# First scores as four 64x32 array tiles issued together, wider third score tile and row-0 product, one matmul for both halves of the gate weights

## The chip, the cores and the metric

The kernel runs on one core of a Trainium2 chip. Its measure is the device time of one launch in microseconds (us): a median over runs, and beside it one execution that was recorded by the profiler. TensorE (PE in the rows) multiplies, VectorE (DVE), ScalarE (ACT) and GpSimd (POOL) work elementwise, SyncE (SP) issues most of the DMAs. Each engine works through its own instruction stream in order and waits on semaphores for the others.

## The reference, cut to what matters

Three stages follow each other: an attention with 32 packed queries per head, a Fourier mixing with a two-layer network, and a mixture of eight experts with one expert per token.

```python
# 8 batches, 8 heads, 576 tokens, head_dim 64, 32 packed queries p
p_packed = sm_attn(p, k, v)                 # first softmax: 32 rows against 576 keys
x = sm_attn(q, p_packed, p_packed)          # second softmax: 576 rows against 32 keys
...
X = np.fft.fft(np.fft.fft(x, axis=1), axis=2)
u = x + np.real(X)                          # then a normalisation of every row
u = u + np.maximum(un @ w_ch1, 0) @ w_ch2   # 512 -> 2048 -> 512
...
logits = u @ w_gate                         # 8 experts, and one column more: w_local
local_gate = sigmoid(u @ w_local)
e = argmax(logits) if s == 0 or local_gate < 0.5 else e_of_the_token_before
out = p[e] * (np.maximum(u @ w1[e], 0) @ w2[e])    # 512 -> 1024 -> 512
```

## The kernel before, in words

**Numbers.** Nearly all products are made of float16 halves: a value is split into hi and lo, and three products (`PASS`: hi*hi, hi*lo, lo*hi) are summed in PSUM. The first scores are the exception: they are float32 matmuls, and each of these shows in the trace as two MATMUL records.

**The generators.** `attention(b)` yields step by step the first softmax, the second softmax, the transforms along channels and sequence, and the normalised rows of one batch. `Mix` is the two-layer network of one group of 512 tokens (256 for the groups "R0" and "R1"): `mm1(f)` makes twelve matmuls into `hp`, `mm2(f)` twelve into the four accumulators `acc`. While the mixing of batch b runs, `tick()` advances `attention(b + 1)`, the splitting of the channel weights (`cw`) and of the expert weights (`ew`: load `se`, split into `so` on ACT at L264 and DVE at L265, write to DRAM), and `after_mix` (scaled rows `xh`, gate logits). At the end come routing and 41 expert blocks (`e1`, `e2`).

**What sets the order.** The code is emitted in that interleaved order, and a scheduler then orders each engine's stream by priority, which is the place of emission; `tc.high_priority(offset=...)` moves instructions forward by so many places. `SOON` is 200 and is given to `greatest` and `exps` of the first softmax; `scores` has offset 0. Tiles of a pool take the slot that comes free, and the first writer of a reused slot waits for the last reader of the old tile.

**The two PSUM slots of `att`.** The pool `psA` has two buffers, which all of these share: the first scores `s1_b_hf_i`, the products `pps`, `ptp`, `s2`, `gp`, `bp`, `zd`, the row tiles `P`, `Q`, `X` of the transforms (`P` of the last 32 slots is read by ACT at L626 and by DVE at L630 to L642, its `X` by DVE at L652), and the logits `lp`. For batch 0 two of three tiles come from `psO` instead.

**The first softmax.** `pt` holds the packed queries of two heads as a block-diagonal 128x64 stationary operand. `scores(hf)` (L367) makes four float32 matmuls of 288 columns, one for each key half i and each pair of heads p2; the outputs of p2 = 0 and 1 stand in partitions 0-63 and 64-127. `greatest` takes maxima on DVE (L378 to L380), `exps` the exponentials on ACT (L385), `turn` casts, splits and transposes by DMA into `et`, which `pps` (L430) multiplies with the values.

**The second scores.** `scores2(i)` (L479) takes the slots in tiles of 128, 128 and 99 (three times the last 32 slots and slot 0), with the queries as stationary operand. `zd` (L572) is the product for row 0, with a stationary operand `zt` of 64 columns. `logits` (L767) makes twelve matmuls of 9 columns a token tile: four row chunks by three passes.

Of the kernel before, what the change touches and what calls it, by code (L numbers as in the profile page):

```python
# [25 lines left out]
RB = 3  # L26


def runs(n):
    """the block of every step: RB runs of blocks take turns, each with weights of its own"""  # L30
    size = [len(range(r, n, RB)) for r in range(RB)]
    return np.array([s // RB + sum(size[:s % RB]) for s in range(n)])


def tokmap():
    """natural token of each (column, partition) of the token tiles"""
# [12 lines left out]
def prep(inputs):  # L49
    """Lays the inputs out for the kernel; the constants depend on shapes alone."""  # L50
# [15 lines left out]
    last = np.concatenate([np.r_[256:288, 0]] * 3)      # the last slots and slot 0, three times  # L66
    o["qd"] = pairs_T(qn[:, :, np.concatenate([np.r_[0:256], last, np.r_[288:544], last + 288])])
    o["kd"] = pairs_T(heads(k))
    pt = pairs_T(heads(p))
    pd = np.zeros((NB, 128, 4, 64), f)  # L70
    pd[:, :64, :, :32] = pt[:, :64]
    pd[:, 64:, :, 32:] = pt[:, 64:]
    o["pd"] = pd
# [20 lines left out]
    # constants from the shapes  # L94
# [27 lines left out]
    c3 = np.zeros((128, 3), f)                          # of the last slots' rows: sign, shift, part  # L122
# [11 lines left out]
    c16[:, 0] = pp[:, None] < pp[None, :]              # strictly earlier rows  # L134
# [48 lines left out]
def _build(tc, nc, ctx, A, stop):  # L183
# [42 lines left out]
    zt = ap.tile([128, 2, 2, 64], F16, name="zt")  # L226
# [40 lines left out]
    def ch_weights():  # L267
        for f in range(16):
# [10 lines left out]
            if srcs[0].dtype == I32:  # L279
                # float64 words to float32: the exponent's three spare bits go, the mantissa keeps 23  # L280
# [18 lines left out]
    def expert_weights():  # L299
        for e in range(NE):  # L300
            for k in range(8):
                # the rows of w1, then those of w2
# [4 lines left out]
                for a in range(2):  # L307
                    so = wp.tile([128, 2, 512], F16, tag="so", name=f"so{e}_{k}_{a}", bufs=2)
                    # no faster than the groups go
# [8 lines left out]
    def attention(b):  # L318
# [8 lines left out]
        def spare(f, n):  # L327
            # room that the weights need later
            return w2h[:, f:f + 3].rearrange("p f a n -> p (f a n)")[:, :n]
# [23 lines left out]
        pt = ap.tile([128, 4, 64], F32, tag="pt", name=f"p{b}")  # L353
# [13 lines left out]
        def scores(hf):  # L367
            s1[hf] = [att(f"s1_{b}_{hf}_{i}") for i in range(2)]
            for i in range(2):
                for p2 in range(2):  # L370
                    nc.tensor.matmul(s1[hf][i][64 * p2:64 * p2 + 64, :288], pt[:, 2 * hf + p2, :],  # L371
                                     kts[hf][:, p2, 288 * i:288 * i + 288], start=True, stop=True)
            (load_v if b else load_q)(hf)
# [23 lines left out]
        for steps in (((scores, 0),), ((greatest, 0),), ((exps, 0), (scores, 1)), ((turn, 0), (greatest, 1)),  # L397
                      ((exps, 1),), ((turn, 1),)):
            for fn, hf in steps:
                with tc.high_priority(offset=SOON if fn in (greatest, exps) else 0):  # L400
                    fn(hf)
# [36 lines left out]
        # every head's own block, divided by the sum  # L438
# [16 lines left out]
        # second softmax, the slots n in tiles of 128, 128 and three times the last 32 and n = 0  # L455
# [4 lines left out]
        # along the channels  # L460
# [18 lines left out]
        def scores2(i):  # L479
            s2 = s2s[i] = att(f"s2_{b}_{i}")  # L480
            for pr in range(4):
                for lu in range(2):
                    c0, j0 = 355 * lu + 128 * i, 256 * lu + 64 * pr
                    for n, (x, y) in enumerate(PASS):
                        nc.tensor.matmul(s2[:nrs[i], j0:j0 + 64], qts[pr // 2][:, x, pr % 2, c0:c0 + nrs[i]],
# [63 lines left out]
        # along the sequence  # L549
        qs0 = ap.tile([128, 576], F32, tag="f32w", name=f"qs{b}_0", bufs=4)  # L550
        for k, (cs, hf) in enumerate(((0, 0), (0, 1), (1, 0), (1, 1))):
# [14 lines left out]
            if k == 2:  # L566
                # row 0: the odd slots' part of P, and what the slots' mean adds
                zd = att(f"zd{b}")
                n = 0
                for hf in range(2):  # L570
                    for (x, y) in PASS:
                        nc.tensor.matmul(zd[:64, :257], zt[:, hf, x], g[:, hf, y, 0], start=n == 0, stop=n == 5)  # L572
                        n += 1
# [3 lines left out]
        for t in (2, 0, 1) if b % 4 == 3 else (0, 1, 2):  # L577
# [76 lines left out]
            if t < 2:  # L654
# [3 lines left out]
                if t == 0 and b % 4 != 3:  # L658
                    # the rest runs beside the next tile
# [58 lines left out]
    class Mix:  # L718
        """one group of tokens: tiles are (U tile, column) of each 128 tokens"""
# [44 lines left out]
    def after_mix(tiles):  # L764
        xt = None

        def logits(col):  # L767
            lp = att(f"lp{col}")
            n = 0
            for c in range(4):  # L770
                for (x, y) in PASS:
                    nc.tensor.matmul(lp[:, :9], xt[:, 4 * x + c], wgh[:, c, y], start=n == 0, stop=n == 11)
                    n += 1
            nc.vector.tensor_scalar(LG[:, col], lp[:, :9], RSC[:, col:col + 1], 2.0 ** -20, ALU.mult, ALU.mult)
# [29 lines left out]
    def choose(gr, rp):  # L804
        """experts of the tokens of four batches, and their weights"""
# [77 lines left out]
        # the weight of the chosen expert, with the scales of the token's row  # L883
# [14 lines left out]
    def place(nm, ncol, b0, nb, early, rp):  # L898
        """blocks b0 .. b0+nb-1 from the tokens of the first ncol columns that are not taken"""
# [28 lines left out]
        # expert of every block  # L928
# [17 lines left out]
        # position of every token  # L946
# [6 lines left out]
        if early:  # L953
# [13 lines left out]
            # the tokens placed here leave the later placement  # L967
# [14 lines left out]
        # the tokens of the slots  # L982
# [253 lines left out]
```

## Time and profile before

| what | value |
|---|---|
| runs: median (lowest to highest) | 1546.48 us (1542.96 to 1549.28), 3 runs |
| profiled execution, first to last instruction (span) | 1548.2 us |
| PE busy | 1422.9 us (92%), 8452 matmul records |
| DVE busy | 771.0 us (50%) |
| ACT busy | 478.3 us (31%) |
| POOL busy | 334.5 us (22%) |
| mean granted TensorE clock, share of full | 0.964 |

The profiled execution has no other time than its span; it lies within the range of the runs. "Busy" is the union of an engine's records. A matmul's record is longer than its share of the stream, since its drain overlaps the next one; so the time that a matmul takes from PE is read from the distance between starts. A row of the timeline merges equal instructions: start, length, engine, line, operation, tiles, count, and in brackets the idle time before it with what ended it. In the rows a tile's buffer numbers are left out: `s` is a score tile of either softmax, told apart by its line.

### The profile page before, as it was taken

Reading aid. Unit: us, or ns where it says so; the run is one execution under the profiler, and the core shown is the slowest. Engines: PE = TensorE matmul, PEld = TensorE weight load, DVE = VectorE, ACT = ScalarE, POOL = GpSimd, SP = SyncE. Lnnn points to the kernel's source line nnn. Section 1 sums busy time; section 2 is a strip of 40 time slices with the busy share of each in tenths; the row PEclk is TensorE's granted clock in tenths of the full one; section 3 lists DMA queues with packets and bytes.
Section 4 is the critical chain, followed back from the end, with each engine's and each line's share of the span. In section 5 each row is a group of like instructions: output and inputs, shape, how many; then the busy total and the mean of one; then the engine's idle time right before and its main releaser. Section 6 shows DMA issues by size and latency. Waiting matters only on the chain. (4 is left out here: it accounts for less than half of the span.)

```text
span 1548.2 us, 23197 instructions
## 1 busy us (share of the span) xinstructions
PE 1422.9 (92%) x8452; PEld 705.5 (46%) x8452; DVE 771.0 (50%) x1547; ACT 478.3 (31%) x892; POOL 334.5 (22%) x332
## 2 busy tenths in 40 slices
PE   4597898998999899999899899999799999989996
PEld 3243444544465454454454456554354344434442
DVE  6778967567564766765766756343441111111110
ACT  4264434335233433533433433211111111111111
POOL 4347414104110410410410420001111121212111
PEclk6589999999999999999999999999999999999999
DMA  8375447457465744836736646244977969897686
GB/s 266 72 231 152 132 109 209 113 138 224 111 167 125 226 118 137 224 104 158 205 105 165 173 123 162 80 164 124 274 181 152 291 134 219 192 318 168 134 201 171
DMA packets 319732, 261.35 MB, mean 169 GB/s; under 512 B 254783, under 2 KB 266175, under 8 KB 318976
## 3 DMA queue, kind: packets, MB, share of 16 engines
q1 hardware_dynamic: 313056, 239.65, 59.5%
q0 software_dynamic: 6560, 20.19, 4.6%
q8 instruction: 67, 1.10, 0.3%
q14 instruction: 49, 0.40, 0.1%
HBM read 267.91 MB, written 53.74 MB: 208 GB/s over the span
## 5 line engine op out<-in xcount | busy, mean ns | idle before, releaser
L753 PE MATMUL acc<-w2h,ht 128*128 128x512 f16 x1728 | 418.4, 382 | 0.6 <-DVE ul L761 0.6
L733 PE MATMUL hp<-ut,w1h 128*128 128x512 f16 x1536 | 377.1, 385 | 6.4 <-DMA ut<-unh 3.5
L733 PEld LDWEIGHTS <-w1h 128*128 128x128 f16 x1920 | 185.0, 99 | 193.7 <-issue 27.1
L753 PEld LDWEIGHTS <-ht 128*128 128x128 f16 x1728 | 165.9, 99 | 195.8 <-issue 22.3
L1098 PE MATMUL ehp<-w1b,xgt 128*128 128x512 f16 x984 | 230.0, 381 | 8.2 <-DMA w1b<-WS 5.8
L1117 PE MATMUL eo<-w2b,hx 128*128 128x512 f16 x984 | 227.4, 381 | 8.7 <-DMA hx<-hb 8.7
L1106 DVE SCALAR_TENSOR_TENSOR hb<-ehp,hb 128x512 f16<-128x512 f32 x82 | 56.7, 691 | 351.4 <-ACT hb L1105 333.9
L741 DVE SCALAR_TENSOR_TENSOR ht<-hp,ht 128x512 f16<-128x512 f32 (+1 forms) x160 | 101.6, 635 | 199.2 <-ACT ht L740 198.4
L1117 PEld LDWEIGHTS <-hx 128*128 128x128 f16 x984 | 95.8, 98 | 126.9 <-DMA hx<-hb 13.9
L1098 PEld LDWEIGHTS <-xgt 128*128 128x128 f16 x984 | 95.7, 98 | 125.4 <-issue 7.1
L264 ACT ACTIVATE so<-se 128x512 f16<-128x512 f32 x128 | 79.8, 627 | 189.8 <-DMA WS<-so 151.6
L740 ACT ACTIVATE ht<-hp 128x512 f16<-128x512 f32 (+1 forms) x160 | 87.4, 547 | 154.6 <-PE hp L733 154.4
L265 DVE SCALAR_TENSOR_TENSOR so<-se,so 128x512 f16<-128x512 f32 x128 | 112.1, 883 | 9.4 <-ACT so L264 9.0
L1124 POOL DMA_INDIRECT out<-ys,sidx x41 | 41.5, 1013 | 326.6 <-ACT ys L1123 291.6
L1123 ACT ACTIVATE ys<-eo,scl 128x512 f32<-128x512 f32 x41 | 28.2, 687 | 266.5 <-PE eo L1117 266.5
L350 POOL TENSOR_TENSOR qh<-q,qh 128x1420 f16<-128x1420 f32 x15 | 43.8, 2921 | 283.9 <-ACT qh L349 281.1
L1068 POOL DMA_INDIRECT xg<-XS,gidx x41 | 42.3, 1031 | 188.2 <-DVE sidx L1024 105.1
L1105 ACT ACTIVATE hb<-ehp 128x512 f16<-128x512 f32 x82 | 48.9, 597 | 105.3 <-PE ehp L1098 105.0
L371 PE MATMUL s<-k,p 128*64 128x288 f32 x128 | 41.1, 466 | 14.6 <-DVE ru L642 9.0
L733 PE MATMUL hp<-utr,w1h 128*128 128x256 f16 x384 | 47.1, 272 | 0.8 <-DVE ht L741 0.8
L557 PE MATMUL bp<-cst,eh 128*128 128x289 f16 (+1 forms) x192 | 35.4, 327 | 13.5 <-ACT eh L534 8.0
L688 POOL TENSOR_TENSOR unh<-un,unh 128x512 f16<-128x512 f32 x32 | 38.1, 1201 | 31.5 <-ACT unh L687 30.2
(287 smaller groups left out, 1388.8 us busy)
## 6 DMA issues: line engine op xcount, KB each, us to landing
w1b<-WS SPq DMA_DIRECT2D x156, 512.0 KB
w2b<-WS SPq DMA_DIRECT2D x156, 512.0 KB
se<-in_w SPq DMA_DIRECT2D x64, 512.0 KB
WS<-so SPq DMA_DIRECT2D x128, 256.0 KB
sw<-in_wc SPq DMA_DIRECT2D x32, 512.0 KB
q<-in_qd SPq DMA_DIRECT2D x16, 710.0 KB
v<-in_vd SPq DMA_DIRECT2D x16, 640.0 KB
k<-in_kd SPq DMA_DIRECT2D x16, 576.0 KB
```

The costliest lines, as they stand in the source:

```text
L264: nc.scalar.activation(dst_hi, src, AF.Copy, scale=scale)
L265: nc.vector.scalar_tensor_tensor(dst_lo, src, scale, dst_hi, ALU.mult, ALU.subtract)
L350: nc.gpsimd.tensor_tensor(qh[:, 1], qt, qh[:, 0], op=ALU.subtract)
L733: nc.tensor.matmul(hp[:, :ntok], w1h[:, f, c, x], ut[:, 4 * y + c, :ntok], start=n == 0, stop=n == 11)
L740: nc.scalar.activation(ht[:, 0, :ntok], hp[:, :ntok], AF.Relu)
L741: pace[0] = nc.vector.scalar_tensor_tensor(ht[:, 1, :ntok], hp[:, :ntok], 0.0, ht[:, 0, :ntok], ALU.max, ALU.subtract).ins
L753: nc.tensor.matmul(self.acc[j], ht[:, x, 128 * j:128 * j + 128], w2h[:, f, y], start=f == 0 and n == 0, stop=f == 15 and n == 2)
L1068: nc.gpsimd.indirect_dma_start(out=g_, out_offset=None, in_=XS[0:rows], in_offset=bass.IndirectOffsetOnAxis(ap=gidx[:, b:b + 1], axis=0), ...
L1098: nc.tensor.matmul(hp, xt[b][:, 4 * x + c], w1b[b % RB][:, 2 * c + fg, y], start=n == 0, stop=n == 11)
L1105: nc.scalar.activation(h[:, fg, :512], hp, AF.Relu)
L1106: nc.vector.scalar_tensor_tensor(h[:, fg, 512:], hp, 0.0, h[:, fg, :512], ALU.max, ALU.subtract)
L1117: nc.tensor.matmul(op, h[:, f // 4, 4 * x + f % 4], w2b[b % RB][:, f, y], start=n == 0, stop=n == 23)
```

## The change

The first scores use `pt` without the zeros: four matmuls of 64 rows and 32 columns in place of two of 128 rows and 64 columns, for each key half. Head r of a pair stands in rows 64r to 64r+63, its output in partitions 64*p2 + 32*r; so the four use two row halves and four column strips, and all write one PSUM tile. `scores` gets the offset `SOON`. The third score tile is computed over 128 columns (29 of them belong to neighbouring slots and are not read), for which the columns of `qd` are laid in another order. `zt` and the row-0 product have 128 columns. The logits take hi and lo of the gate weights as one operand of 18 columns for the hi rows and 9 columns for the lo rows; DVE then adds the two halves. Comments were removed throughout.

```diff
-    o["qd"] = pairs_T(qn[:, :, np.concatenate([np.r_[0:256], last, np.r_[288:544], last + 288])])
+    o["qd"] = pairs_T(qn[:, :, np.concatenate([np.r_[0:256], last + 288, last, np.r_[288:544]])])
...
-    pd = np.zeros((NB, 128, 4, 64), f)
-    pd[:, :64, :, :32] = pt[:, :64]
-    pd[:, 64:, :, 32:] = pt[:, 64:]
-    o["pd"] = pd
+    o["pd"] = pairs_T(heads(p))
...
-    zt = ap.tile([128, 2, 2, 64], F16, name="zt")
+    zt = ap.tile([128, 2, 2, 128], F16, name="zt")
...
-        pt = ap.tile([128, 4, 64], F32, tag="pt", name=f"p{b}")
+        pt = ap.tile([128, 4, 32], F32, tag="pt", name=f"p{b}")
...
             for i in range(2):
                 for p2 in range(2):
-                    nc.tensor.matmul(s1[hf][i][64 * p2:64 * p2 + 64, :288], pt[:, 2 * hf + p2, :],
-                                     kts[hf][:, p2, 288 * i:288 * i + 288], start=True, stop=True)
+                    for r in range(2):
+                        d, row = slice(64 * r, 64 * r + 64), 64 * p2 + 32 * r
+                        nc.tensor.matmul(s1[hf][i][row:row + 32, :288], pt[d, 2 * hf + p2],
+                                         kts[hf][d, p2, 288 * i:288 * i + 288], start=True, stop=True)
...
-                with tc.high_priority(offset=SOON if fn in (greatest, exps) else 0):
+                with tc.high_priority(offset=SOON if fn in (scores, greatest, exps) else 0):
...
-                    c0, j0 = 355 * lu + 128 * i, 256 * lu + 64 * pr
+                    c0, j0 = ((0, 128, 355), (454, 582, 256))[lu][i], 256 * lu + 64 * pr
                     for n, (x, y) in enumerate(PASS):
-                        nc.tensor.matmul(s2[:nrs[i], j0:j0 + 64], qts[pr // 2][:, x, pr % 2, c0:c0 + nrs[i]],
+                        nc.tensor.matmul(s2[:, j0:j0 + 64], qts[pr // 2][:, x, pr % 2, c0:c0 + 128],
...
-                        nc.tensor.matmul(zd[:64, :257], zt[:, hf, x], g[:, hf, y, 0], start=n == 0, stop=n == 5)
+                        nc.tensor.matmul(zd[:, :257], zt[:, hf, x], g[:, hf, y, 0], start=n == 0, stop=n == 5)
...
             for c in range(4):
-                for (x, y) in PASS:
-                    nc.tensor.matmul(lp[:, :9], xt[:, 4 * x + c], wgh[:, c, y], start=n == 0, stop=n == 11)
-                    n += 1
-            nc.vector.tensor_scalar(LG[:, col], lp[:, :9], RSC[:, col:col + 1], 2.0 ** -20, ALU.mult, ALU.mult)
+                nc.tensor.matmul(lp[:, :18], xt[:, c], wgh[:, c].rearrange("p y e -> p (y e)"), start=c == 0, stop=False,
+                                 skip_group_check=True)
+                nc.tensor.matmul(lp[:, :9], xt[:, 4 + c], wgh[:, c, 0], start=False, stop=c == 3, skip_group_check=True)
+            lsum = wp.tile([128, 9], F32, tag="lsum", name=f"lsum{col}", bufs=2)
+            nc.vector.tensor_reduce(lsum, lp[:, :18].rearrange("p (y e) -> p e y", y=2), axis=AX.X, op=ALU.add)
+            nc.vector.tensor_scalar(LG[:, col], lsum, RSC[:, col:col + 1], 2.0 ** -20, ALU.mult, ALU.mult)
```

The offset moves the scores on PE. Before, the scores of batch 3 stand in the mixing of group 8 (batch 2), third product of `mm1`; each float32 matmul stands between two of the mixing's:

```order
L733 MATMUL hp8_2_3160<-ut2_2809,w1h_127 128x512
L371 MATMUL s1_3_0_0_3176<-k3_0_3172,p3_3169 64x288
L733 LDWEIGHTS w1h_127
L733 MATMUL hp8_2_3160<-ut2_2809,w1h_127 128x512
L371 MATMUL s1_3_0_0_3176<-k3_0_3172,p3_3169 64x288
```

After, they stand in the last product of the group before it (`hp4_15`), twelve matmuls `acc4` to `acc7` behind the transform's last row tiles `P2_2` and `X2_2`:

```order
L753 MATMUL acc7_2049<-w2h_128,ht4_12_2913 128x512
L370 MATMUL s1_3_0_0_3192<-k3_0_3188,p3_3185 32x288 x4
L733 LDWEIGHTS w1h_127
L733 MATMUL hp4_15_3078<-ut1_1693,w1h_127 128x512
...
L370 MATMUL s1_3_0_1_3193<-k3_0_3188,p3_3185 32x288 x4
...
L370 MATMUL s1_3_1_0_3238<-k3_1_3190,p3_3185 32x288 x4
L370 MATMUL s1_3_1_1_3239<-k3_1_3190,p3_3185 32x288 x4
```

Four matmuls of the mixing stand between the first two groups of scores, seven between the second and the third, none between the third and the fourth. Batches 5, 6 and 7 have the same order; in batch 2 ten matmuls stand ahead of the first group, and two between it and the second; batch 4's scores move by half a product only. The first group writes the slot of `P2_2`, the second that of `X2_2`, the third and fourth the slots of the first two.

On ACT the copy of `P2_2` (`qs2_2`) and the exponentials of batch 3 stand like this before:

```order
L264 ACTIVATE so1_0_0_3067<-se1_0_3050 128x512
L626 COPY qs2_2_3045<-P2_2_3016 32x257
L264 ACTIVATE so1_0_1_3084<-se1_0_3050 128x512
L264 ACTIVATE so1_1_0_3209<-se1_1_3167 128x512
L740 ACTIVATE ht4_15_3080<-hp4_15_3062 128x512
L264 ACTIVATE so1_1_1_3247<-se1_1_3167 128x512
```

and after:

```order
L260 ACTIVATE so1_0_0_3083<-se1_0_3066 128x512
L626 COPY qs2_2_3061<-P2_2_3032 32x257
L260 ACTIVATE so1_0_1_3100<-se1_0_3066 128x512
L260 ACTIVATE so1_1_0_3229<-se1_1_3183 128x512
L384 ACTIVATE e32_3_0_3235,sums3_3187<-s1_3_0_0_3192,mx3_0_3217 128x288
L384 ACTIVATE e32_3_0_3235,sums3_3187<-s1_3_0_1_3193,mx3_0_3217 128x288
```

The splits `so` of the expert weights stay ahead of the copy; the exponentials now come behind the third of them, ahead of `ht4_15`.

## Rows read from the trace of the kernel before

**Rows 1.** Stretch: length; PE, PEld, DVE, ACT, POOL busy (records); clock, DMA share, GB/s.
```profile
217.00:332.00 115.00, 109.57 (x712) 54.09 (x710) 74.40 (x143) 44.38 (x84) 24.19 (x24) 0.99 0.58 157
```

**Rows 2.** Timelines of ACT, PE, DVE behind the last row tiles of batch 2.
```profile
314.46 0.63 ACT L264 ACTIVATE so<-se 128x512 f16<-128x512 f32 x1 [2.00 <-DMA WS<-so]
320.87 0.63 ACT L264 ACTIVATE so<-se 128x512 f16<-128x512 f32 x1 [3.08 <-DMA WS<-so]
315.14 2.54 PE L733 MATMUL hp<-ut,w1h 128*128 128x512 f16 x11
316.87 0.41 DVE L642 TENSOR_TENSOR ru<-P,qs 32x256 f32<-32x256 f32 x1
```

**Rows 3.** Timeline of PE, scores of batch 2 in steady mixing.
```profile
216.75 0.70 PE L371 MATMUL s<-k,p 128*64 128x288 f32 x2
217.39 0.39 PE L733 MATMUL hp<-ut,w1h 128*128 128x512 f16 x1
217.71 0.70 PE L371 MATMUL s<-k,p 128*64 128x288 f32 x2
```

**Rows 4.** Timeline of PE, all scores of batch 0, at the lower clock.
```profile
5.50 4.18 PE L371 MATMUL s<-k,p 128*64 128x288 f32 x16 [5.50 <-DMA k<-in_kd]
```

**Rows 5.** Timeline of PE, column tiles and two score matmuls side by side.
```profile
63.79 0.28 PE L609 MATMUL X<-pph,big 128*32 128x256 f16 x2
64.00 0.71 PE L371 MATMUL s<-k,p 128*64 128x288 f32 x4
```

**Rows 6.** Timeline of PE, second scores of batch 1.
```profile
121.60 1.56 PE L485 MATMUL s<-pth,qh 128*128 128x64 f16 x48
126.89 1.27 PE L485 MATMUL s<-pth,qh 128*99 128x64 f16 x24
```

**Rows 7.** Timeline of PE, one logits product; then DVE's group that reads them.
```profile
856.63 0.45 PE L772 MATMUL lp<-wgh,xt 128*128 128x9 f16 x12
856.94 2.75 PE L733 MATMUL hp<-ut,w1h 128*128 128x512 f16 x12
L774 DVE TENSOR_SCALAR LG<-lp,RSC 128x9 f32<-128x9 f32 x36 | 7.8, 217 | 12.0 <-PE lp L772 11.8
```

**Rows 8.** Groups of PE by form: the row-0 product.
```profile
L572 PE MATMUL zd<-g,zt 128*64 128x257 f16 x48 | 7.4, 295 | 1.1 <-DVE zt L564 1.1
```

**Rows 9.** Timelines of PE and DVE at the same place of batches 1, 5, 6.
```profile
199.83 0.38 PE L733 MATMUL hp<-ut,w1h 128*128 128x512 f16 x1
200.76 0.40 DVE L642 TENSOR_TENSOR ru<-P,qs 32x256 f32<-32x256 f32 x1
...
700.89 2.75 PE L733 MATMUL hp<-ut,w1h 128*128 128x512 f16 x12
704.67 0.40 DVE L642 TENSOR_TENSOR ru<-P,qs 32x256 f32<-32x256 f32 x1
...
815.68 2.54 PE L733 MATMUL hp<-ut,w1h 128*128 128x512 f16 x11
817.51 0.41 DVE L642 TENSOR_TENSOR ru<-P,qs 32x256 f32<-32x256 f32 x1
```

**Rows 10.** Timeline of SP, the second load of batch 3's keys.
```profile
249.43 0.85 SPq L360 DMA_DIRECT2D k<-in_kd  x1
```

**Rows 11.** Timeline of PE, waits ahead of the products with the values.
```profile
349.30 1.03 PE L430 MATMUL pps<-vhl,et 128*64 128x128 f16 x30 [1.78 <-DMA et<-ehl]
855.01 1.03 PE L430 MATMUL pps<-vhl,et 128*64 128x128 f16 x30 [1.79 <-DMA et<-ehl]
```

**Rows 12.** A wait of PE, and busy times of stretches around it and another.
```profile
534.38 0.64 PE L468 MATMUL gp<-cdt,pth 128*64 128x257 f16 x6 [2.12 <-DVE ee L494]
344.00:356.00 12.00, 10.22 (x99) 5.19 (x97) 7.92 (x15) 8.10 (x14) 2.50 (x1) 1.00 1.08 297
529.00:541.00 12.00, 9.88 (x74) 4.75 (x73) 11.38 (x22) 4.57 (x9) 7.54 (x9) 0.86 0.48 118
```

**Rows 13.** Waits over 217 to 860 us: who for whom, total, times, longest.
```profile
ACT so L264 <- DMA WS<-so: 115.8, 58, 6.7
```

More of the change, by code (lines that the diff above doesn't have):

```diff
@@ L66, in prep @@
     last = np.concatenate([np.r_[256:288, 0]] * 3)
-    o["qd"] = pairs_T(qn[:, :, np.concatenate([np.r_[0:256], last, np.r_[288:544], last + 288])])
+    o["qd"] = pairs_T(qn[:, :, np.concatenate([np.r_[0:256], last + 288, last, np.r_[288:544]])])
     o["kd"] = pairs_T(heads(k))
-    pt = pairs_T(heads(p))
-    pd = np.zeros((NB, 128, 4, 64), f)
-    pd[:, :64, :, :32] = pt[:, :64]
-    pd[:, 64:, :, 32:] = pt[:, 64:]
-    o["pd"] = pd
+    o["pd"] = pairs_T(heads(p))
     vv = heads(v).transpose(0, 2, 1, 3).reshape(NB, S, D)
@@ L768, in logits @@
             lp = att(f"lp{col}")
-            n = 0
             for c in range(4):
-                for (x, y) in PASS:
-                    nc.tensor.matmul(lp[:, :9], xt[:, 4 * x + c], wgh[:, c, y], start=n == 0, stop=n == 11)
-                    n += 1
-            nc.vector.tensor_scalar(LG[:, col], lp[:, :9], RSC[:, col:col + 1], 2.0 ** -20, ALU.mult, ALU.mult)
+                nc.tensor.matmul(lp[:, :18], xt[:, c], wgh[:, c].rearrange("p y e -> p (y e)"), start=c == 0, stop=False,
[4 more added lines that the diff above has]
+            nc.vector.tensor_scalar(LG[:, col], lsum, RSC[:, col:col + 1], 2.0 ** -20, ALU.mult, ALU.mult)
         for j, (ut, col) in enumerate(tiles):
```

## The prediction

> **What bounds the kernel now.** I read the table of stretches first, then the timeline of PE where the change acts, then ACT and DVE beside it. In the stretch from 217 to 332 us, which the later batches repeat, PE is busy for 109.6 of 115 us at a granted clock of 0.99, DVE for 74.4, ACT for 44.4 [rows 1]. So PE's stream sets the end there, and what the change takes from it comes off the total as long as PE doesn't wait for something new. Batches 0 and 1 run before the mixing is in step, and there I count PE time for little.
>
> **The scores.** A matmul of the mixing takes 0.22 us of the stream (eleven of them 2.54 us, the last one's drain included [rows 2]). A score matmul stands between two of them: from one score to the next it is 0.96 us [rows 3], so the score itself takes 0.96 - 0.22 = 0.74 us, or 8 x 0.74 = 5.9 us a batch. What of that is streaming is seen in batch 0, where eight float32 matmuls lie in each column half and the two halves side by side: 4.18 us at the lower clock [rows 4], 0.52 for each of the two records of a matmul, so about 0.26 at full clock and 0.5 for both. The other 0.24 us is the change of shape and the first load, paid each time a score stands alone. Outputs in different column strips do run side by side: two 32-column products start at the same 0.01 us, and four records of two scores take 0.71 us together, as one score does alone [rows 5]. The new scores add the second dimension, two row halves, which no row shows. I take it that all four tiles run together. A group of four then takes 0.74 us, and the fourth group, right behind the third, 0.5: 3 x 0.74 + 0.5 = 2.7 us a batch. Batches 2, 3, 5, 6, 7 gain 5.9 - 2.7 = 3.2 us each, together 16.0. In batch 4 two pairs already stood side by side, so before it was 6 x 0.74 = 4.4 and the gain is 1.7. Batch 1 has the same 1.7 on paper, but stands where PE waits for others; I take 1.0 (0 to 3). Batch 0 gains nothing: each tile has a stream of eight records as before.
>
> **A rule against it.** The rows show column strips side by side, all at 128 rows [rows 5]. The Trainium skill, "TensorEngine Tiling (Array Packing)", section "Restrictions and Gotchas", says that different row tiles cannot use the same PSUM bank at once; here both row halves write one score tile. No trace of before can show it. By that rule the case is the second rival below.
>
> **The other edits.** Third score tile: 24 matmuls of 99 columns take 1.27 us, 48 of 128 columns 1.56 [rows 6], so 24 would take 0.78; the difference of 0.49 holds one drain too many, and I take 0.44, times 8 batches 3.5 us. Logits: from the first of twelve to the next matmul it is 0.31 us [rows 7], 0.026 each; four fewer for each of 36 token tiles is 144 x 0.026 = 3.7 us (the wider 18 columns are still far below what one costs; if they cost double, 0). DVE adds a reduction for each, about as long as the 0.22 us of the scaling [rows 7], 8 us in all; DVE has a third of its time free [rows 1], and only the last tiles before the second routing would show it, under 1 us. Row-0 product: six matmuls a batch at 7.4 / 48 = 0.154 us [rows 8], where 257 columns stream in 0.11; the excess of 2.1 us in all is the most that can go, I take 0.5.
>
> **The wait that is added.** This is the other half of the sum. With the new offset the scores of batches 2, 3, 5, 6, 7 come some 120 matmuls of the mixing earlier, 120 x 0.22 = 26 us, right behind the last row tiles P and X of the batch before, and their first matmul writes P's slot. PE executes in order, so all the mixing behind it waits with it. Before, at the point where the first group now stands, PE goes on with `hp` at 315.14, while DVE's last read of P ends at 316.87 + 0.41 = 317.28 [rows 2]: 2.1 us of waiting for batch 3. The reason stays: on ACT the copy of P stands behind a split `so` that waited 2.00 us for its write DMA [rows 2], and the new order keeps it there. The same subtraction gives 1.8 us for batch 2 (whose place is two matmuls earlier than the `hp` row), 4.2 for batch 6 and 2.2 for batch 7 [rows 9]; batch 5 I take like batch 7. Sum 12.5. The second group needs X's slot, which DVE frees two adds later; 0.74 us of scores and four matmuls of the mixing cover that. The third needs the first exponential: in batch 3 ACT's third split ends at 321.50 [rows 2], and PE is there at 317.28 + 2 x 0.74 + 11 x 0.22 = 321.2, so with the exponential itself about 1 us more. In all 13.5 us. The loads are no new wait: batch 3's keys are issued by 249.4 [rows 10], 60 us before. The load of the values goes out behind the scores, earlier than before, and only ACT's cast waits for it.
>
> **What goes away beside.** Products with the values waited for the transposed exponentials three times in the later batches, 1.78 and 1.79 us in batches 3 and 7 [rows 11] and about as long in 4. For 3 and 7 the exponentials now come long before, and nothing else of that product is later: 3.6 us. Batch 4's come a little earlier: 0.8. Together 4.4.
>
> **The clock.** A wait of 1.78 us left the granted clock at 1.00 over the 12 us around it; one of 2.12 is followed by 0.86 [rows 11, 12], which costs 0.14 x 12 = 1.7 us. Of the five new waits four are over 2 us. I count three drops, 5 us (0 to 8.5).
>
> **The sum.** Gains 16.0 + 1.7 + 1.0 + 3.5 + 3.7 + 0.5 + 4.4 = 30.8; losses 13.5 + 5 = 18.5; net -12. The profiled execution spans 1548.2 us, 1.7 above the median of the runs; I apply the -12 to the median of 1546.48 and forecast 1535 us. Own range 1525 to 1545: the new waits anywhere between 1.0 and 4.5 us a place, the clock between no drop and five.
>
> **Rivals.**
> First, the early scores cost nothing: with less work ahead, DVE and ACT are done with P in time. For it: P's own chain is a copy and four reads of 0.4 us, less than the twelve matmuls ahead take. Against it: the split that stands ahead waits for a DMA, which no faster PE shortens. Then the gains stand alone, 1546.5 - 30.8 = 1516.
>
> Second, the two row halves take turns because they write one score tile: each group takes 0.5 us longer, 1.9 a batch, 11.5 for batches 2 to 7, 2.5 in batch 1 and, at the lower clock, 3.8 in batch 0. The forecast becomes 1535 + 17.5 = 1552. If all four tiles ran one after another it would be some 50 us more. Against it: column strips are seen side by side, and the outputs lie in different partitions.
>
> Third, slower: the wait for P's slot outgrows everything, since it hangs on ACT's split and so on a write DMA. The longest such wait was 6.7 us, the mean 115.8 / 58 = 2.0 [rows 13]. With 6.7 at each of the five places a wait grows by 4.7 to some 7 us, 35 in all with five drops of the clock: 30.8 - 35 - 8.5 = 13 more than before, 1559. It decides from the point where P comes free 4.4 us after PE is there (30.8 less 8.5, by five); in the rows it is 1.8 to 4.2.
>
> **How the numbers follow.** A measurement of this kernel tells about 0.5% from no change, 7.7 us: faster means below 1538.7, slower above 1554.2. Chances: forecast 0.55, first rival 0.20, second 0.13, third 0.12. Of the forecast's own range two thirds lie below 1538.7, so faster is 0.37 + 0.20 = 0.57; the rest of the forecast, most of the second rival and a little of the third lie within 0.5%, 0.30; slower is 0.13. The range for 8 times in 10 goes from 1517, next to the first rival, to 1554, past the second.
>
> **What would show it.** Four records of a group start within 0.02 us and a group takes about 0.74; two steps of starts 0.5 us apart would be the second rival. In front of the first group of batches 2, 3, 5, 6, 7 stands idle time of 1.5 to 4.5 us that ends with DVE's read of P at L642; none there is the first rival, 6 and more the third. The third score tile's run of 24 should take 0.9 us, a logits product 0.2 us of the stream, and the waits ahead of the values' products of batches 3 and 7 should be gone. I am wrong if the scores' group costs more than 1 us, or if PE's gain is taken back by a wait that I have not listed.

## The result, and the profile after

The changed kernel took 1530.5 us (median of 4 runs, 1523.4 to 1533.6) against 1546.7 us for the kernel before in the same series: ratio 0.9881, 95% interval 0.9847 to 0.9914. A second series gave 1528.6 against 1551.8 us, ratio 0.9863 (0.9839 to 0.9888). The forecast was 1535 us with a range of 1517 to 1554.

Three stages make up the time: the start (up to the first matmul of the mixing), the mixing stage with the attention of the later batches inside it, and the expert stage. The table of stretches for the last two, of after (columns as in [rows 1]):

```profile
76.00:1048.60 972.60, 919.39 (x6024) 467.36 (x6024) 623.96 (x1277) 372.36 (x701) 223.28 (x205) 0.98 0.55 155
1048.60:1517.60 469.00, 444.55 (x2100) 202.24 (x2099) 90.62 (x200) 78.72 (x129) 79.07 (x77) 0.99 0.85 207
```

The same two stretches of before:

```profile
78.50:1074.40 995.90, 944.50 (x6048) 479.09 (x6048) 625.21 (x1245) 368.75 (x701) 223.44 (x205) 0.98 0.55 152
1074.40:1536.40 462.00, 442.36 (x2116) 202.54 (x2115) 90.14 (x196) 78.70 (x129) 78.60 (x77) 0.99 0.87 210
```

The mixing stage is 23.3 us shorter. PE is busy 25.1 us less in it, and its idle time (length less busy) goes from 51.4 to 53.2. The start gives 2.5 us. The expert stage, whose code is the same, is 7 us longer in these two traces; a second trace of after has 461.7 there, so the 7 us are scatter between executions of one program (below). The timeline of PE at batch 7's scores, which answers to [rows 3], and at the third score tile of batch 1, which answers to [rows 6]:

```profile
797.37 0.69 PE L370 MATMUL s<-k,p 64*32 64x288 f32 x8 [2.21 <-issue]
797.99 1.04 PE L733 MATMUL hp<-ut,w1h 128*128 128x512 f16 x4
798.95 0.69 PE L370 MATMUL s<-k,p 64*32 64x288 f32 x8
...
125.51 0.86 PE L485 MATMUL s<-pth,qh 128*128 128x64 f16 x24
```

Eight records (four tiles of two) take 0.69 us together, and the next matmul starts 0.62 us after the first of them. The first records of the four tiles start within 0.02 us. Each record by itself is 0.40 us long (the view of that line over 797 to 798 us: number, least, median and greatest ns, first and last start):

```profile
L370 PE MATMUL s<-k,p x8: 399/402/427, 797.4 to 797.7; 64*32 64x288 f32 x8
```

Eight times 0.40 in 0.69 us can only be if all four tiles run at once. Before, a lone column tile, with two records, cost 0.64 us in the same measure [rows 3]: 216.75 to 217.39.

A logits product, first and last record and the next matmul, answers to [rows 7]; the products with the values of batches 3 and 7 answer to [rows 11]. PE's timeline:

```profile
833.27 0.17 PE L770 MATMUL lp<-wgh,xt 128*128 128x18 f16 x1
...
833.45 0.17 PE L772 MATMUL lp<-wgh,xt 128*128 128x9 f16 x1
833.47 0.81 PE L733 MATMUL hp<-ut,w1h 128*128 128x512 f16 x3
...
339.66 1.03 PE L429 MATMUL pps<-vhl,et 128*64 128x128 f16 x30
831.65 1.03 PE L429 MATMUL pps<-vhl,et 128*64 128x128 f16 x30
```

Logits are at 0.20 us, and both waits for the transposed exponentials are gone. The new wait is the last thing to read. Timelines of ACT, DVE and PE behind batch 4's last row tiles, ahead of batch 5's scores, which answer to [rows 2]:

```profile
571.45 0.63 ACT L260 ACTIVATE so<-se 128x512 f16<-128x512 f32 x1 [2.02 <-DMA WS<-so]
572.28 0.63 ACT L260 ACTIVATE so<-se 128x512 f16<-128x512 f32 x1 [0.21 <-DMA WS<-so]
572.94 0.37 ACT L626 COPY qs<-P 32x257 f32<-32x257 f32 x1
...
573.34 0.41 DVE L630 TENSOR_TENSOR rl<-P,qs 32x256 f32<-32x256 f32 x1 [3.19 <-ACT qs L626]
...
574.34 0.40 DVE L642 TENSOR_TENSOR ru<-P,qs 32x256 f32<-32x256 f32 x1
...
574.84 0.81 PE L370 MATMUL s<-k,p 64*32 64x288 f32 x8 [2.58 <-issue]
```

The group starts 0.1 us after DVE's last read of P ends, so the wait is the one that was forecast, although the profile puts it down to "issue". PE's waits ahead of the scores from 196 us on (total, times, longest) are those at the five places:

```profile
PE s L370 <- issue: 9.0, 4, 2.6
PE s L370 <- DVE ru L642: 2.9, 1, 2.9
```

### The profile page after: what moved, and what is told of

It is laid out like the page before. It is cut to its first block, busy times and chain, and to the rows that moved or that the text cites. A ratio compares the mean times of both kernels' runs of the same rounds, so it can differ in the third digit from the quotient of the medians.

```text
span 1529.1 us, 23161 instructions
## 1 busy us (share of the span) xinstructions
PE 1396.3 (91%) x8436; PEld 690.6 (45%) x8436; DVE 769.7 (50%) x1583; ACT 482.2 (32%) x892; POOL 335.8 (22%) x332
## 5 line engine op out<-in xcount | busy, mean ns | idle before, releaser
L753 PE MATMUL acc<-w2h,ht 128*128 128x512 f16 x1728 | 414.0, 382 | 0.8 <-DVE ul L761 0.8
L1118 PE MATMUL eo<-w2b,hx 128*128 128x512 f16 x984 | 229.7, 383 | 14.6 <-DMA hx<-hb 14.1
L261 DVE SCALAR_TENSOR_TENSOR so<-se,so 128x512 f16<-128x512 f32 x128 | 100.0, 790 | 10.3 <-ACT so L260 10.3
L370 PE MATMUL s<-k,p 64*32 64x288 f32 x256 | 24.8, 488 | 27.0 <-DVE ru L642 12.3
L557 PE MATMUL bp<-cst,eh 128*128 128x289 f16 (+1 forms) x192 | 33.0, 312 | 14.1 <-DVE g L472 5.9
```

The source lines that it names most:

```text
L261: nc.vector.scalar_tensor_tensor(dst_lo, src, scale, dst_hi, ALU.mult, ALU.subtract)
L753: nc.tensor.matmul(self.acc[j], ht[:, x, 128 * j:128 * j + 128], w2h[:, f, y], start=f == 0 and n == 0, stop=f == 15 and n == 2)
L1118: nc.tensor.matmul(op, h[:, f // 4, 4 * x + f % 4], w2b[b % RB][:, f, y], start=n == 0, stop=n == 23)
```

## The experiments

All in one table first. Lengths come from the table of stretches; where a kernel has two traces, both are given. Two traces of one program differ by up to 5 us in the mixing stage and up to 15 us in the expert stage (10 to 12), so smaller differences between single traces tell nothing.

| kernel | ratio to before (95%) | mixing stage, us | PE busy in it | idle in it | expert stage |
|---|---|---|---|---|---|
| before | 1 | 995.9, 998.6 | 944.5, 944.2 | 51.4, 54.5 | 462.0, 463.2 |
| after (two series) | 0.9881 (0.9847 to 0.9914), 0.9863 (0.9839 to 0.9888) | 972.6, 971.9 | 919.4, 915.4 | 53.2, 56.5 | 469.0, 461.7 |
| 1, 11: no score part | 0.9988 (0.9961 to 1.0015), 0.9988 (0.9967 to 1.0009) | 995.7, 990.8 | 936.9, 931.6 | 58.9, 59.2 | 476.3, 461.2 |
| 2: early place, column tiles, rest | 0.9899 (0.9838 to 0.9960) | 975.6 | 920.2 | 55.4 | 466.6 |
| 3: four tiles, old priority | 1.0030 (1.0003 to 1.0058) | 999.2 | 934.8 | 64.5 | 468.9 |
| 4: first group 15 matmuls later | 0.9873 (0.9810 to 0.9937) | 978.0 | 919.2 | 58.8 | 470.9 |
| 5: four tiles together, old place | 0.9904 (0.9877 to 0.9931) | 981.6 | 919.4 | 62.2 | 461.6 |
| 6: early place alone | 0.9946 (0.9925 to 0.9966) | 988.7 | 931.1 | 57.6 | 462.9 |
| 7: three so buffers | 0.9955 (0.9937 to 0.9973) | 982.9 | 916.3 | 66.7 | 469.8 |
| 8: P's slot free early | 0.9867 (0.9831 to 0.9904) | 970.5 | 915.9 | 54.6 | 466.7 |
| 9: column tiles together alone | 1.0017 (0.9999 to 1.0036) | 989.6 | 931.2 | 58.4 | 474.7 |

**1. Without the score part.** The scores of before, at their old place; the rest of the change stays.

```diff
-                with tc.high_priority(offset=SOON if fn in (scores, greatest, exps) else 0):
+                with tc.high_priority(offset=SOON if fn in (greatest, exps) else 0):
...
-                    for r in range(2):
-                        d, row = slice(64 * r, 64 * r + 64), 64 * p2 + 32 * r
-                        nc.tensor.matmul(s1[hf][i][row:row + 32, :288], pt[d, 2 * hf + p2],
-                                         kts[hf][d, p2, 288 * i:288 * i + 288], start=True, stop=True)
+                    nc.tensor.matmul(s1[hf][i][64 * p2:64 * p2 + 64, :288], pt[:, 2 * hf + p2, :],
+                                     kts[hf][:, p2, 288 * i:288 * i + 288], start=True, stop=True)
```

> The change without its score part: scores as 128x64 column tiles at their old place, only the third score tile, the row-0 product and the logits as in the kernel after. Theory A (the score part brings most: its stream time 13.8 us, and earlier exponentials that shorten later waits by some 8 us, less 12 us of the new wait and some 5 us of lower clock): what is left is 3.4 + 2.9 + 0.8 = 7.1 us of stream time, so 1539 us (1536 to 1542). Rival B (the shorter waits ahead of the second scores and the channels come from the third tile and the logits, not from earlier exponentials): 7.1 + 8.5 = 15.6 us, so 1531 us.

Measured: 1549.5 us, ratio 0.9988, no change that can be told. Neither theory: PE's busy time did fall by 8 us in this trace, but idle time rose by 7.

**2. The place alone.** As 1, with `scores` in the list of line 399 again, so that the two 128x64 column tiles of a group are issued next to each other at the early place.

> The scores at the early place of the kernel after, but as before in two 128x64 column tiles (pairs issued together). Theory A: a batch's scores cost 4.2 us (the 16 records of batch 0 before) in place of 5.9, so six batches gain some 10 us; the wait on P's slot costs its 12 us and the clock some 5 as in the kernel after, and later waits shrink by some 8: about 1 us below the kernel without the score part, 1538 us (1535 to 1541). Rival C (the place alone brings it, the packing is hidden): 1531 us, as the kernel after.

Measured: 1534.6 us, between A's 1538 and C's 1531; by the time alone the two are not told apart (the ratio's interval spans 19 us). Against 1, whose time A had put 10 us too low, the early place with its pairs gains 15 us. PE's rows at batch 7 here:

```profile
804.53 0.71 PE L372 MATMUL s<-k,p 128*64 128x288 f32 x4
805.16 0.60 PE L735 MATMUL hp<-ut,w1h 128*128 128x512 f16 x2
```

0.63 us from the pair to the next matmul, where after has 0.62 for four tiles and before 0.64 for a single one.

**3. The tiles alone.**

```diff
-                with tc.high_priority(offset=SOON if fn in (scores, greatest, exps) else 0):
+                with tc.high_priority(offset=SOON if fn in (greatest, exps) else 0):
```

> The four 64x32 array tiles at the old priority: no early place, and about half of the score groups are spread singly between other matmuls. Theory A: a single score matmul between others costs some 0.5 us, so a batch costs 8 x 0.5 + 2 x 0.65 = 5.3 us against 5.9; no wait on P's slot; six batches gain 3.5 us over the kernel without the score part: 1535 us (1532 to 1539), and the waits of later steps as without the score part. Rival D (the packing brings all by itself, wherever it stands): 1530 us or less, since it has no wait on P's slot.

Measured: 1555.9 us, slower than before by 0.3% (0.0 to 0.6). Both theories are wrong: A forecast a small gain over 1 and D a large one, and the run is 6 us slower than 1. PE's rows where a small tile stands alone:

```profile
833.04 0.67 PE L370 MATMUL s<-k,p 64*32 64x288 f32 x2
833.64 0.39 PE L733 MATMUL hp<-ut,w1h 128*128 128x512 f16 x1
833.96 0.67 PE L370 MATMUL s<-k,p 64*32 64x288 f32 x2
```

A lone 64x32 tile costs 0.60 us, as much as four. The groups of score matmuls over the whole run (busy us, mean ns of one, then idle time before), of before, after, 2 and 3 in turn:

```profile
L371 PE MATMUL s<-k,p 128*64 128x288 f32 x128 | 41.1, 466 | 14.6 <-DVE ru L642 9.0 <-DMA k<-in_kd 5.5
```
```profile
L370 PE MATMUL s<-k,p 64*32 64x288 f32 x256 | 24.8, 488 | 27.0 <-DVE ru L642 12.3 <-issue 9.0 <-DMA k<-in_kd 5.5
```
```profile
L372 PE MATMUL s<-k,p 128*64 128x288 f32 x128 | 25.7, 504 | 26.2 <-DVE ru L644 11.7 <-issue 8.9 <-DMA k<-in_kd 5.6
```
```profile
L370 PE MATMUL s<-k,p 64*32 64x288 f32 x256 | 45.4, 452 | 15.0 <-DVE ru L642 9.3 <-DMA k<-in_kd 5.7
```

So standing together is worth 15.4 us of PE time to the column tiles (41.1 to 25.7). Four tiles in place of two are worth another 0.9 by these rows; by starts (time from each matmul's start to the next one, summed over the mixing stage) 2 and after have 17.7 and 17.8 us. That the four tiles bring anything over the pair is not shown.

**4. The wait taken away by order.** In batches 2, 3, 5, 6, 7 the first score group may not pass a given matmul of the mixing stream (`pe` lists them). In the trace it stands 15 matmuls later than after (17 in batch 2), not 19.

```diff
+                        with tc.issue_after(pe[-64]) if b in (2, 3, 5, 6, 7) and hf == i == 0 else nullcontext():
                             nc.tensor.matmul(s1[hf][i][row:row + 32, :288], pt[d, 2 * hf + p2],
```

> The kernel after with one edit: in batches 2, 3, 5, 6 and 7 the first score group may not be issued before a given matmul of the mixing stream, which puts it 19 matmuls (some 4.1 us) later in TensorE's queue, still four tiles together, and behind the release of P's slot (2.1 to 2.9 us). Theory A (the idle ahead of the first group is time lost on the critical path, and three clock drops of 1.7 us follow from it): 11.9 + 5 us less, 1514 us (1510 to 1519), the five idle stretches under 0.3 us, and no clock drop at them. Rival W (the mixing stage is bound by the ScalarE and VectorE chain there, and what isn't waited for ahead of the scores is waited for ahead of a later step): 1527 to 1531 us, with new idle time ahead of pps, second scores or channels.

Measured: 0.9873, as after within the interval; theory W. The waits ahead of the first groups are gone, but in three batches the third group now waits for its slot until the first exponentials are done, and the channels wait longer: 9.3 us behind `ee`, `lsum` and `g`, against 2.1 in after. The mixing stage is 5 us longer than in after. PE's waits from 196 us on:

```profile
PE s L370 <- ACT e L384: 7.8, 3, 2.8
...
PE gp L467 <- DVE ee L494: 3.5, 3, 2.6
PE gp L467 <- DVE lsum L774: 2.9, 3, 1.5
```

**5. Together, at the old place.** Experiment 4 with `pe[-1]`: the first group stands where it stood before, which by the trace is 78 matmuls later than after (80 in batch 2), not 65.

> The kernel after with one edit: in batches 2, 3, 5, 6 and 7 the score groups are held back to within a few rows of their place of before, some 65 matmuls (14 us) later, but stay four tiles together. Stream time of the scores as after (17.8 us in the mixing stage, not 31.6), no wait on P's slot. Theory S (issuing together is what counts; stream time saved is time saved): 13.8 below the kernel without the score part (1549), and no wait of 12: 1535 us or less. Theory E (the attention chain from the exponentials on sets the stage, so what counts is when the scores run; TensorE time saved elsewhere comes back as idle time ahead of pps, channels and bp): as the kernel without the score part, 1545 to 1549 us, with idle time in the mixing stage of 65 us or more against 53 after.

Measured: 1534.1 us, theory S for the total. The mixing stage says more: it is 9 us longer than after with the same PE busy time. The waits of PE from 196 us on, of 5 and then of after, for the steps that follow the exponentials:

```profile
PE s L485 <- DVE pth L451: 11.3, 6, 3.0
PE pps L429 <- DMA et<-ehl: 2.9, 5, 1.1
PE s L485 <- ACT pth L450: 2.7, 2, 2.3
PE gp L467 <- DVE ee L494: 1.5, 2, 1.0
PE gp L467 <- DVE lsum L774: 1.5, 2, 0.8
```
```profile
PE pps L429 <- DMA et<-ehl: 1.9, 1, 1.9
PE s L485 <- ACT pth L450: 1.9, 1, 1.9
PE gp L467 <- DVE ee L494: 0.9, 1, 0.9
PE s L485 <- DVE pth L451: 0.4, 1, 0.4
```

19.9 us against 5.1. This is what the early place buys, and it pays 11.9 for it at P's slot; the rest of the 9 us is in smaller waits, the largest of them 3.0 ahead of the transposes `ptp`.

**6. The early place, nothing else.** One line of before:

```diff
-                with tc.high_priority(offset=SOON if fn in (greatest, exps) else 0):
+                with tc.high_priority(offset=SOON if fn in (scores, greatest, exps) else 0):
```

> The kernel before with one edit: the scores at the early place. Third score tile, row-0 product and logits as before, so 7 us more of stream time than in the run with the place alone (1534.6). Theory E: those 7 us are hidden in the chain's waits, as they were in the run without the score part: 1533 to 1537 us. Theory S: 1541 us.

Measured: 1542.1 us, theory S: third tile, row-0 product and logits are worth something here (from 6 to 2: PE busy 10.9 us less, idle 2.2 less, mixing stage 13.1 shorter), where in 1 the stage was 4 us shorter by the means of two traces and the total showed nothing that can be told.

**7. A third buffer for so.**

Beside what the diff shows, the tiles that share `so`'s tag get `bufs=3`, and five small constants move to the pool `ap`.

```diff
-                    so = wp.tile([128, 2, 512], F16, tag="so", name=f"so{e}_{k}_{a}", bufs=2)
+                    so = wp.tile([128, 2, 512], F16, tag="so", name=f"so{e}_{k}_{a}", bufs=3)
...
-        ppr = ap.tile([128, 2, 128], F32, tag="pp1", name=f"ppr{b}")
+        ppr = ap.tile([128, 2, 128], F32, tag="t16", name=f"ppr{b}")
```

> The kernel after with a third buffer for the expert weights' halves (so), paid for by letting ppr share a buffer with t16 and moving five small constants to another pool. ScalarE's copies of the expert weights then wait less for their own writes to DRAM, and what stands behind them in ScalarE's queue comes earlier. Theory E (the ScalarE and VectorE chain sets the stage): the mixing stage shortens by 4 to 10 us, 1521 to 1527 us; the wait ahead of the first score group falls to some 2.0 us where it was 2.6 to 2.9, and stays at 2.1 in batch 2, where no so stands ahead of it. Rival (so's wait is beside the chain): 1530 us.

Measured: 1542.8 us, slower than after; both theories wrong. ACT's group of these copies (busy, mean ns, then idle time before it by what ended it), of 7 and then of after:

```profile
L260 ACT ACTIVATE so<-se 128x512 f16<-128x512 f32 x128 | 80.2, 628 | 228.4 <-DMA se<-in_w 110.9 <-DMA WS<-so 99.0 <-DVE mv L676 6.2
```
```profile
L260 ACT ACTIVATE so<-se 128x512 f16<-128x512 f32 x128 | 79.5, 628 | 181.9 <-DMA WS<-so 159.7 <-issue 6.8 <-DVE un L683 5.1
```

The wait for the writes shrank and a wait for the loads took its place. The copies stand earlier in ACT's queue now, one more of them ahead of nearly every step of the attention, so ACT stands longer in front of data that isn't there, with the attention's steps behind it. That this is what made the kernel slower is argued, not shown: `ppr` shares its buffer with other tiles now, and no run separates the two. The wait at P's slot is gone in batch 5, 1.7 and 1.4 us in batches 6 and 7 and 2.9 as in after in batch 3, but channels wait more (of PE, from 196 us on):

```profile
PE gp L467 <- DVE ee L494: 4.3, 3, 3.2
PE gp L467 <- DVE lsum L774: 4.2, 3, 2.2
```

**8. P's slot free early.** DVE copies P beside ACT's copy of the other product, and reads the copy afterwards; the first group is issued 10 matmuls later.

```diff
+            if t == 2 and b in (1, 2, 4, 5, 6): nc.vector.tensor_copy(qs[R, 288:545], P[R, :257]); P = qs[:, 288:545]
...
+                        with tc.issue_after(pe[-69]) if b in (2, 3, 5, 6, 7) and hf == i == 0 else nullcontext():
```

> The kernel after with two edits for batches 2, 3, 5, 6 and 7: VectorE copies the third tile's P to SBUF beside ScalarE's copy of the other product, so that P's slot is free after one copy (0.4 us) instead of four reads (1.6 us); and the first score group is issued 10 matmuls (2.2 us) later, so that it meets a free slot. In time it starts no later than after. Theory A (the idle ahead of the first group is lost time): idle there under 0.3 us each, 12 us and some clock drops less: 1514 to 1519 us. Theory E: the exponentials start about 1 us earlier per batch, and that is the gain: 1524 to 1528 us, the rest comes back as idle time ahead of pps, second scores and channels.

Measured: 1527.1 us, theory E's figure. There is no wait ahead of the first groups, but the second ones wait for X's slot, which DVE frees two adds later. PE's waits again:

```profile
PE s L370 <- DVE rl L652: 7.9, 5, 2.3
```

It is the shortest mixing stage of all (970.5), and cannot be told from after by its time (0.9867 and 0.9863 to 0.9881).

**9. Column tiles together, nothing else.** Experiment 6 with the gate of 5: before, with only the pairs put side by side near their old place.

> The kernel before with one edit, to the order of TensorE's queue alone: the two 128x64 column tiles of a score group are issued next to each other, in batches 2, 3, 5, 6 and 7 within a few rows of their place of before (batches 1 and 4 a little earlier). No four tiles, no early place, third tile, row-0 product and logits as before. Theory S (a lone column tile takes as long as a pair, so issuing the pair together halves the stream time of the scores, 31.6 to 16 or 18 us, and that is the gain): 1549.6 - 14 = 1536 us (1533 to 1540). Theory E (where the scores start is what counts): 1547 to 1551 us.

Measured: 1553.0 us in 12 runs (1550.2 to 1560.5), theory E's side. PE is busy 13 us less, idle time is 4 to 7 us up, and the mixing stage is 6 to 9 us shorter, so half of S's gain was there. The total doesn't show it: the expert stage of this trace is 474.7 us, with 17.9 us of waiting for its second product's transposes (`hx`) where the two traces of before have 8.7 and 9.7.

**10, 11, 12. After, no score part, and before once more.**

> The kernel after once more, for a second trace and a tighter interval. If the lengthening of the expert stage (462 to 469 us between the two first traces) belongs to the change, it is there again, 468 us or more, and the ratio is 0.988; if it is chance, the stage lies anywhere between 461 and 471 us and the ratio may come nearer to 0.984, which the mixing stage alone would give.

> The kernel without the score part once more. Theory S (stream time saved is time saved): 7 us below before, ratio 0.9955. What the first run showed (7 us of stream time less, and 7 us of idle time more in the mixing stage, ratio 0.9988): 0.9988 again, with the idle time again at 57 us or more, most of the growth ahead of the channels step.

> The kernel before, for a second trace: how far idle time in the mixing stage (51 us in the first trace) and the length of the expert stage (462 us) move between two executions of the same program. If both repeat within 2 us, differences of 5 us and more between kernels belong to the kernels.

Measured: after 1528.6 us, 0.9863, expert stage 461.7; without the score part 0.9988 again, idle 59.2 us; before 998.6 us of mixing, with idle time 3.1 and the expert stage 1.2 us above the first trace, the first of these more than the 2 us that were expected. The two traces without the score part (the second first) show where their idle time grew, in the channels' group of PE (idle time behind the second bar), which had 9.4 and 9.6 before:

```profile
L469 PE MATMUL gp<-cdt,pth 128*64 128x257 f16 x192 | 16.6, 286 | 13.5 <-DVE ee L496 7.5 <-DVE g L474 2.9 <-DVE lsum L776 2.7
```
```profile
L469 PE MATMUL gp<-cdt,pth 128*64 128x257 f16 x192 | 16.8, 288 | 15.2 <-DVE ee L496 6.6 <-DVE lsum L776 5.3 <-DVE g L474 2.9
```

The logits' new reduction (`lsum`) holds the slots that channels need, 2.7 and 5.3 us where its forerunner `LG` took 0.9 and 1.9 before; that shows in 4, 5 and 7 too, where the waits for it are 2.9, 1.5 and 4.2, and not in after. Mixing stages repeat within 5 us, those of before and after within 3. The expert stage doesn't: one and the same program had 469.0 and 461.7, another 476.3 and 461.2. More than half of that is waiting on its second product's transposes: 14.1 us for `hx` in the first trace of after, 10.0 in the second, and 18.1 and 9.7 without the score part. The granted clock of the stage is lower in the longer trace of each, 0.99 against 1.00 and 0.98 against 0.99. The row of the first in the profile's page:

```profile
L1118 PE MATMUL eo<-w2b,hx 128*128 128x512 f16 x984 | 229.7, 383 | 14.6 <-DMA hx<-hb 14.1 <-SPq L1211 0.4
```

So a difference of under 15 us between the totals of two single traces says nothing here; one of more than 5 us between mixing stages does.

## Why the prediction was right, and where it was not

The time fell inside the range and near the forecast. By its own steps:

**PE's stream sets the end.** Half right. The stage is 23 to 27 us shorter for 25 to 29 us of PE time. But "what the change takes from it comes off the total as long as PE doesn't wait for something new" failed: some 6 of 10 us of PE time saved in 1 (mean of two traces) and some 5 of 13 in 9 came back, in 1 for some 3 us behind the new reduction `lsum`, and for the rest in waits that were there already. In 9 the second scores' wait for `pth` grew from 7 to 14 us. The chain from the exponentials over `pth` to channels runs on ACT and DVE, and a shorter PE stream meets it earlier. Of the mixing stage, 1 takes 4 us and 9 takes 8, both savings together take 15 at the old place (5), and 25 with the early place.

**The scores.** The cost of a group was right (0.62 us to the next matmul, by the measure that gave 0.64 for a lone one), and so, nearly, was the saving: 16.3 us by the groups of the profile's page (41.1 to 24.8) where 18.7 were forecast with batches 1 and 4; by starts it is 13.8 (31.6 to 17.8), 14.8 in the second trace of after, where 17.7 were forecast for the batches in the mixing stage. What it was put down to was not separated. The row that shows two scores in the time of one [rows 5] was in hand, and it meant that the old column tiles, issued together, would save as much. Experiments 2 and 3 show it: the saving is that the tiles stand together, and the early priority is what puts them together. The two row halves add 0.9 us at most by the first traces. The move is smaller than the prediction has it: by the traces the first group comes 78 matmuls earlier, not 120, which no term of the sum used, and in batch 2 four matmuls of the mixing stand between the first two groups, not two.

**The rule against it** (second rival). The Trainium skill, "TensorEngine Tiling (Array Packing)", "Restrictions and Gotchas", would have the row halves not use one PSUM bank at once. The trace does not agree for this case: four tiles of two row halves, in one score tile at different partitions, took 0.69 us for 8 records of 0.40, all four starting within 0.02 us. The rival, whose parts add up to 17.8 us and not 17.5, is out.

**The other edits.** Third tile 0.86 us, logits 0.20 us, as forecast. By starts they gave 2.9, 3.4 and the row-0 product 0.8, 7.1 together, 7.7 forecast. That they reach the end was not a matter of course: 1 shows some half of it in its stage, which is within the scatter, and nothing in its total; 2 against 6 shows all of it.

**The added wait.** 13.5 us forecast, 11.9 measured in both traces, at the five places named. That the sum is so near is in part luck: batch 6 waits 2.1 us where 4.2 were forecast, batch 3 2.9 for 2.1, and the 1 us for the third group's slot did not come. The reason given was half right: batch 2 waits 2.1 us (1.5 in the second trace) with no split right ahead of the copy, so much of it is the copy and DVE's four reads, 0.37 and 1.4 us. In the other four batches a split that waited for its write stands ahead; 7, where that wait shrank, has no wait in batch 5, with one split fewer ahead of the copy, 0.4 and 0.8 us less in 6 and 7, and as much as after in batch 3. That the early scores cost nothing (first rival, 1516 us) did not happen, and that the wait's removal would be worth its length is refuted by 4 and 8: the wait went to a later slot.

**What goes away beside: the step that was mis-sized.** Forecast 4.4 us, from the waits for `et` alone, and those did fall by 4.1. But the other idle time in the mixing stage as a whole fell by 10 us (51.4 to 53.2 with 11.9 new in it; 54.5 to 56.5 in the second traces), since the early exponentials help the second scores and channels too, which the forecast left out. PE's waits of before from 196 us on, against those of after that stand at experiment 5:

```profile
PE s L485 <- DVE pth L452: 7.1, 6, 2.0
PE pps L430 <- DMA et<-ehl: 6.0, 5, 1.8
PE s L485 <- ACT pth L451: 0.4, 1, 0.4
```

The two waits for `pth` went from 7.5 to 2.3 us. In 5, with the work of after but late exponentials, they are 14.0.

**The clock.** Three of the five waits have a lower clock around them in the first trace, as counted, those of batches 3, 5 and 6; in the second trace, with the same 11.9 us of waits, only that of batch 7 (2.2 us) has, and batch 3's, the longest with 3.6 us, stands in a stretch at 1.00. Around two of the first (12 us each):

```profile
570.00:582.00 12.00, 9.42 (x57) 2.88 (x56) 5.14 (x13) 3.58 (x9) 0.07 (x1) 0.86 0.55 164
303.00:315.00 12.00, 9.02 (x69) 3.12 (x71) 5.48 (x13) 3.74 (x9) 1.30 (x2) 0.86 0.69 160
```

But the mean granted clock of the execution is 0.966 and 0.972 after and 0.964 and 0.965 before, since drops elsewhere went: before, the clock over 383 to 395 us was 0.72, and 0.86 in the second trace at that place; after, it is 1.00 in all of 332 to 450 us in both traces. (That of [rows 12] did not go: after has 0.86 over 507 to 519 us, at the second scores of the same batch.) The 5 us were not lost on balance. This term and the one before it are what the forecast of -12 us lacked; with 10 for 4.4 and 0 for 5 it would have been -23. Measured are -16 and -23 by the medians of the two series, -18 and -21 by their ratios.

**Slower by P's slot** (third rival): no wait over 2.9 us in the first trace and 3.6 in the second, and it needed 4.4 on average. Out.

What stays open: why 9 is not faster in all, with a mixing stage 6 to 9 us shorter. Its expert stage was long by its waits for `hx`, which in 1 went from 18.1 to 9.7 us between two traces of one program; but 12 runs in a row make chance alone unlikely, and no run here separates the causes. What makes 7 slow is not separated either, and 8 against after is below what these runs can tell.

## What to carry to other kernels

Before you pack smaller tiles, look whether the tiles you have are issued next to each other: a lone one can cost what a full group costs. Time saved on the busiest engine reaches the end only if the chain on the others is ahead at that place, so look which old waits will grow; and moving work early can pay for its own new wait. A wait that is taken away at one slot of a two-buffer pool can be met again at a later slot, and one more buffer may only move an in-order queue's wait from the writes to the loads.

## What the runs showed of the hardware

A float32 score matmul between two of another shape costs 0.60 us as a 64x32 tile, 0.64 us as a 128x64 tile, 0.63 us as a pair of these and 0.62 us as four 64x32 tiles; a second group right behind the first adds only about 0.5, as the forecast had it: this row of 9 has two groups of one pair each, 712.78 to 713.91 us, in 1.13. All of these have 288 columns and stand in stretches with a granted clock of 1.00.

```profile
712.78 1.19 PE L371 MATMUL s<-k,p 128*64 128x288 f32 x8
713.91 0.39 PE L733 MATMUL hp<-ut,w1h 128*128 128x512 f16 x1
```
